# Eighteen products of the last output projection moved into the last slot, their bank, and the queue of the last sums

## The chip, the cores and the metric

One Trainium2 chip, one core. The metric is the device time in microseconds (us) of one execution of the program. Before the change three runs gave 1958.81, 1959.34 and 1960.34 us, a median of 1959.34 us. Engines are named as in the profile: PE (TensorE), PEld (its weight loads), DVE (VectorE), ACT (ScalarE), POOL (GpSimd), SP (SyncE, here only a DMA queue).

## The reference

Two attention blocks read the same input x (2048 x 512, 32 heads of 16) and are mixed row by row with a gate. Cut to what matters:

```
g = sigmoid((x * gate_w).sum(-1))
# A: causal softmax attention inside each of 4 segments of 512 rows, mixed with a linear memory of the earlier segments
o = sigmoid(beta) * a_mem + (1 - sigmoid(beta)) * softmax(q k^T / 4 + mask) v
a = o @ A_wo
# B: full softmax attention over 2048 keys
b = (softmax(q k^T / 4) v) @ B_wo
out = g * a + (1 - g) * b
```

The last output projection is the product of the normalised, gated o of both blocks (512 + 512 columns) with A_wo and B_wo.

## The kernel before

**Units and slots.** Attention is cut into 64 units: 32 of A (4 segments x 8 quarters of the heads, unit k) and 32 of B (4 chunks of 512 query rows x 8 quarters of 4 heads, unit 32 + k). Slot k of the main loop (L932 to L966) does B's unit 32 + k and A's unit k. In a slot, n runs over 37 groups (NG): groups 0 to 31 are B's, two per key tile of 128 keys, and 32 to 36 are A's. A group (`t_group`, L516) makes two score tiles of 128 x 512 on PE, one for each half of the array's rows, into two PSUM banks, and ACT takes the exponential of each tile out of its bank (L534) into `raw`. `pv` (L540) then multiplies the exponentials with the values and adds up in the bank `pvb`; in slot 31 (L860) it does so once per key tile, after the odd group, one key tile behind. The instructions of every engine stand in the order in which this code issues them.

**Banks.** PSUM has eight banks here: `tb` (two, TB), `mb`, `pvb`, and `sbk` (two tiles of two banks). `bank` (L88) hands out the allowed bank that was used longest ago. In slots 0 to 30 the scores use T3 = TB + [MB], and `sbk` holds other score tiles, of which only the row maximum is taken (L452 to L476, reduced on DVE). Slot 31 has no next unit to take maxima for, so its groups rotate over five banks, T3 and the first halves of the two `sbk` tiles (L934). The small jobs (`misc`, L95) also take theirs from T3: in slot 31 these are two halves of an earlier output projection, `out_mm(22)` after group 1 and `out_mm(23)` after group 28 (12 products each, L616, taken out by ACT L620 and by DVE L623), and `m_rows` (L501) after group 24.

**Output.** Each sum o·W is made of three products of split operands (high and low parts, TERMS). For the last 512 rows (c = 3), the tail does the projection: t counts four tiles of 128 rows, `tail_mm(t, gs, a)` (L639) adds the products of head groups gs and block a (0 is A, 1 is B) into the bank TAIL[t]. Of its 24 products a tile, 18 (head groups 0 to 2) need nothing of the last slot; their operands are split on DVE during the slot's first groups (L911). The other 6 need group 3, which waits for the units 63 and 31.

**The end of the last units.** `fin_copy` (L553) copies `pvb` to `pvs` (ACT L559) and stores it to DRAM (L561). For unit 63 the sums are loaded again (L567, L569), inverted on DVE (L574, L578), stored (L580) and loaded back in 64 rows (L586, `d<-rd`); POOL multiplies (L590), then SP loads the memory part (L593, `d<-om`). For unit 31, SP loads the denominators (L971) and sums (L972); the loop at L983 inverts and multiplies on DVE (L986 to L988), adds the memory part on POOL (L989), and splits (ACT L634, POOL L637). B's group 3 is split on DVE (L636, L637) at L980. `tail_out` (L646) copies the four banks out by halves and stores them.

## Time and profile before

| | us |
|---|---|
| median of three runs | 1959.34 |
| the profiled execution, its own time | 1956.4 |
| its span in the profile | 1954.7 |
| last slot, from its first score tile to the last product of pvb | 1883.69 to 1928.25 |
| tail, from there to the last product on PE | 1928.25 to 1950.76 |
| last copy out of PSUM and last stores | 1950.86 to 1954.7 |

The profiled execution took 1956.4 us, 1.7 us more than its span, and lay 2.9 us under the median of the runs. Times in rows are us from the start of the span. A row of the chain of waits says where the path to the last instruction ran; a row of the timeline says when an instruction started, how long it took, and in square brackets how long its engine had been idle and which instruction ended that. Matmul rows merge several instructions (x4); their ends overlap with the next row's start.

### The profile page before, as it was taken

The numbers are of one execution on the slowest core, as the hardware profiler recorded it, in microseconds if no ns is written. First come the engines' busy times: TensorE is split into PE (matmuls) and PEld (weight loads), VectorE is DVE, ScalarE is ACT, GpSimd is POOL, SyncE is SP. The second block draws the span as 40 slices with busy tenths as digits, with TensorE's granted clock in tenths as the row PEclk, the third lists the DMA queues.
The fourth block names the chain that finished last, engine by engine and source line by source line (L and its number), as shares of the span: only waits on it lengthen the run. The fifth ranks groups of instructions, "written<-read, shape, count | busy, mean of one in ns | idle before, by whom it ended". The sixth has DMA issues, their size and how long they took to land.

```text
span 1954.7 us, 43539 instructions
## 1 busy us (share of the span) xinstructions
PE 1930.3 (99%) x17485; PEld 939.3 (48%) x17485; DVE 1629.9 (83%) x1798; ACT 1433.4 (73%) x2699; POOL 275.8 (14%) x497
## 2 busy tenths in 40 slices
PE   7999999999999999999999999999999999999999
PEld 5887777444344444444444444444444444444445
DVE  7135766899999999999999999999999999999942
ACT  4233333688888888888888888888888888888884
POOL 5201000012120101111111111111111111111022
PEclk9999999999999999999999999999999999999999
DMA  7666655644444444343435453444354444434111
GB/s 218 170 205 188 198 192 178 156 98 115 98 115 93 106 91 109 81 111 80 114 87 115 87 115 87 113 87 115 87 115 87 109 86 96 101 88 106 48 50 58
DMA packets 163790, 222.49 MB, mean 114 GB/s; under 512 B 39916, under 2 KB 90556, under 8 KB 157828
## 3 DMA queue, kind: packets, MB, share of 16 engines
q1 hardware_dynamic: 159284, 211.41, 43.7%
q0 software_dynamic: 3248, 8.03, 2.1%
q8 instruction: 138, 2.26, 0.5%
q14 instruction: 64, 0.52, 0.1%
q10 hardware_dynamic: 1056, 0.26, 0.1%
HBM read 147.95 MB, written 68.16 MB: 111 GB/s over the span
## 4 chain that ended last, share of the span: by engine, by line
PE 95%; DVE 3%; ACT 1%; SPq 1%; DMA 1%; issue 0%; DVEq 0%; ACTq 0%
PE pvb L550 33%; PE tb L528 17%; PE sbk L474 12%; PE mb L528 9%; PE tb L304 4%; PE sbk L452 3%; PE tb L616 2%; PE mb L304 2%; PE sbk L287 1%; DVE mxb L476 1%; PE tb L287 1%; PE pvb L304 1%; PE mb L616 1%; PE sbk L456 1%; PE mb L287 1%; PE pvb L287 1%
## 5 line engine op out<-in xcount | busy, mean ns | idle before, releaser
L476 DVE TENSOR_REDUCE mxb<-sbk 128x2 f32<-128x1024 f32 x1024 | 1222.3, 1222 | 67.3 <-PE sbk L474 63.1
L534 ACT ACTIVATE raw<-tb 128x512 f32<-128x512 f32 x1555 | 887.5, 598 | 152.9 <-PE tb L528 89.6
L550 PE MATMUL pvb<-raw,vb 128*17 128x256 f32 (+1 forms) x8072 | 639.3, 388 | 0.0
L534 ACT ACTIVATE raw<-mb 128x512 f32<-128x512 f32 x782 | 467.6, 598 | 79.5 <-PE tb L528 44.8
L528 PE MATMUL tb<-qb,xh 64*128 64x512 f32 x872 | 331.6, 495 | 1.7 <-ACT raw L534 1.7
L550 PEld LDWEIGHTS pvb<-raw,vb 128*17 128x17 f32 x8072 | 134.4, 95 | 340.1 <-issue 336.6
L474 PE MATMUL sbk<-xh,qb 64*128 64x512 f32 x1344 | 281.5, 395 | 2.7 <-DVE mxb L476 1.8
L528 PE MATMUL mb<-qb,xh 64*128 64x512 f32 x445 | 220.6, 496 | 0.0
L537 POOL TENSOR_SCALAR_AFFINE_SELECT raw<-raw 128x256 f32<-128x256 f32 (+1 forms) x320 | 115.5, 361 | 709.6 <-ACT raw L534 701.7
L528 PEld LDWEIGHTS tb<-qb,xh 64*128 64x128 f32 x872 | 124.7, 183 | 179.6 <-issue 89.9
L528 PE MATMUL tb<-qb,kb 64*128 64x512 f32 x470 | 179.5, 496 | 1.3 <-DVE st L314 0.8
L460 DVE TENSOR_REDUCE mx<-sbk 128x2 f32<-128x768 f32 (+1 forms) x128 | 136.7, 1090 | 22.9 <-PE sbk L456 18.3
L474 PE MATMUL sbk<-kb,qb 64*128 64x512 f32 x704 | 146.4, 398 | 0.0
L474 PEld LDWEIGHTS sbk<-xh,qb 64*128 64x128 f32 x1344 | 138.3, 186 | 7.4 <-DVE mxb L476 5.0
L528 PEld LDWEIGHTS mb<-qb,xh 64*128 64x128 f32 x445 | 81.3, 183 | 95.2 <-issue 50.4
L590 POOL TENSOR_TENSOR o<-o,d 128x512 f32<-128x512 f32 x31 | 39.7, 1281 | 545.6 <-DMA d<-rd 461.9
L528 PEld LDWEIGHTS tb<-qb,kb 64*128 64x128 f32 x470 | 68.2, 183 | 100.1 <-issue 52.6
L528 PE MATMUL mb<-qb,kb 64*128 64x512 f32 x234 | 116.1, 496 | 0.0
L550 PE MATMUL pvb<-raw,va 128*17 128x256 f32 (+2 forms) x1280 | 94.7, 384 | 0.8 <-ACT pvs L559 0.8
L452 PE MATMUL sbk<-ka,qa 64*128 64x256 f32 (+3 forms) x512 | 88.2, 358 | 1.1
L528 PE MATMUL tb<-qa,ka 64*128 64x512 f32 (+3 forms) x339 | 79.5, 372 | 0.0
L311 ACT ACTIVATE st<-tb 128x512 fp32r<-128x512 f32 x33 | 19.8, 599 | 80.2 <-DVE phi L310 40.5
(284 smaller groups left out, 1837.6 us busy)
## 6 DMA issues: line engine op xcount, KB each, us to landing
xh<-dB SPq DMA_DIRECT2D x38, 512.0 KB
vb<-vdB SPq DMA_DIRECT2D x16, 1088.0 KB
dB<-st SPq DMA_DIRECT2D x64, 256.0 KB
dA<-st SPq DMA_DIRECT2D x64, 256.0 KB
pd<-pvs SPq DMA_DIRECT2D x64, 256.0 KB
kb<-dB SPq DMA_DIRECT2D x22, 512.0 KB
xh<-dB SPq DMA_DIRECT2D x38, 256.0 KB
qb<-dB SPq DMA_DIRECT2D x64, 128.0 KB
```

Source lines behind the costliest of these rows:

```text
L287: nc.tensor.matmul(b, lhs, WV[wi][:, k, :], start=n == 0, stop=n == 11)
L304: nc.tensor.matmul(b, WS[ws][w][wi][:, k, :], (XH, XL)[xi][c][:, k, :], start=n == 0, stop=n == 11)
L452: nc.tensor.matmul(b[:, j, c0:c0 + n], q_of(u)[r, p, i * 128:(i + 1) * 128], k_of(u, p)[r, :n], start=True, stop=False)
L460: nc.vector.tensor_reduce(m[:, :, p, i], b[:, :, :n], axis=AX.X, op=OP.max)
L474: nc.tensor.matmul(b[:, j], q_of(u)[r, p, i * 128:(i + 1) * 128], k_of(u, p)[r, kc * C:(kc + 1) * C], start=True, stop=True)
L476: nc.vector.tensor_reduce(MXB[u][:, :, p, i, kc], b, axis=AX.X, op=OP.max)
L528: nc.tensor.matmul(bs[j][:, c0:c0 + w], k_of(u, h // 2)[r, 128 * it:128 * it + 128], q_of(u)[r, h // 2, q0:], start=True, stop=True)
L534: nc.scalar.activation(pt, bs[j], AF.Exp, scale=SCALE)
L537: nc.gpsimd.affine_select(out=m, in_=m, pattern=[[1, 128]] if n < 2 else [[0, 2], [1, 128]], compare_op=OP.is_ge, fill=0.0, base=0, channe ...
L550: nc.tensor.matmul(PVB[32 * h:32 * h + E + 1, q0 + lo:q0 + hi], vt[:, it, 4 * q + h, :], pt[:, lo:hi], start=it == 0 and lo == 0, stop=it ...
L590: nc.gpsimd.tensor_tensor(o, o, d, op=OP.mult)
L616: nc.tensor.matmul(b, (AT["oh"], AT["ol"])[oi][:, g, a], (AT["wh"], AT["wl"])[wi][:, g, a], start=n == 0, stop=n == 11)
```

## The change

Three things, all of them in the last slot and behind it:

1. Tile t = 0 of the last projection gets `mb` as its bank, and its first 18 products run inside slot 31, six of them (one head group, both blocks) between the two score groups of a key tile, at n = 8, 14 and 20. The score groups of slot 31 rotate over four banks in place of five, without `mb`, and the small jobs of that slot over TB alone.
2. The store of unit 31's `pvs` and the two loads behind it are issued by ACT's queue, not SP's.
3. DVE normalises tiles 0 and 1 of unit 31 ahead of splitting B's group 3; the normalising of tiles 2 and 3 lies between those splits.

```
-        nc.sync.dma_start(AT["pd", u].rearrange("h r t -> (h r) t"), ps)
+        (nc.scalar if u == 31 else nc.sync).dma_start(AT["pd", u].rearrange("h r t -> (h r) t"), ps)
...
-    TAIL = T3 + [SBK[0][:, 0]]
+    TAIL = [MB] + TB + [SBK[0][:, 0]]
...
+        if k == 31:
+            for g in range(3):
+                pre[8 + 6 * g] = [todo(tail_mm, 0, (g,), a) for a in range(2)]
...
-        banks = T3 + [b[:, 0] for b in SBK] * (k == 31)
+        banks = T3 if k < 31 else TB + [b[:, 0] for b in SBK]
+        if k == 31:
+            mode["misc"] = TB
...
-    nc.sync.dma_start(den, AT["pd", 31][:, E:E + 1].to_broadcast([4, E, C]))
-    nc.sync.dma_start(AT["o"][1][64:, 3, 0], AT["pd", 31][:, :E])
-    for t in range(2):
+    nc.scalar.dma_start(den, AT["pd", 31][:, E:E + 1].to_broadcast([4, E, C]))
+    nc.scalar.dma_start(AT["o"][1][64:, 3, 0], AT["pd", 31][:, :E])
+    for t in range(1, 4):
         for a in range(2):
             tail_mm(t, range(3), a)
-    for a in range(2):
-        tail_mm(2, range(3), a)
     fin_norm("B", 3, 3)
+
+    def last_norm(t):
+        d = den[:, t * 128:(t + 1) * 128]
+        o = o_cols(3, t)[64:, 3, 0]
+        nc.vector.reciprocal(d, d)
+        nc.vector.tensor_tensor(d, d, AT["grest"][:, t * 128:(t + 1) * 128], op=OP.mult)
+        nc.vector.tensor_tensor(o, o, d, op=OP.mult)
+
+    def last_add(t):
+        o = o_cols(3, t)[:, 3, 0]
+        nc.gpsimd.tensor_tensor(o, o, AT["d"][1][:, t * 128:(t + 1) * 128], op=OP.add)
+        tail_split(t, slice(3, 4), 0, nc.gpsimd)
+
+    for t in range(2):
+        last_norm(t)
     for t in range(4):
         tail_split(t, slice(3, 4), 1)
-    for a in range(2):
-        tail_mm(3, range(3), a)
-    for t in range(4):
-        d = den[:, t * 128:(t + 1) * 128]
-        o = o_cols(3, t)[:, 3, 0]
-        nc.vector.reciprocal(d, d)
-        nc.vector.tensor_tensor(d, d, AT["grest"][:, t * 128:(t + 1) * 128], op=OP.mult)
-        nc.vector.tensor_tensor(o[64:], o[64:], d, op=OP.mult)
-        nc.gpsimd.tensor_tensor(o, o, AT["d"][1][:, t * 128:(t + 1) * 128], op=OP.add)
-        tail_split(t, slice(3, 4), 0, nc.gpsimd)
+        if t < 2:
+            last_add(t)
+        else:
+            last_norm(t)
+            last_add(t)
```

Behind that point the file's lines shift: what was L971, L972, L986 to L989 in the kernel before is L976, L977, L986 to L988 and L992 in the changed one.

**PE at the start of slot 31.** The rows are `out_mm(22)` (L616) behind group 1, and the score groups 2 and 3 behind it (L528); tb_110 and tb_111 are the two banks of TB, sbk_114 and sbk_115 the two halves of `sbk`. Before:

```order
L528 MATMUL tb_111<-qb_68,xh_87 128x512
L528 MATMUL tb_110<-qb_68,xh_87 128x512
L616 MATMUL mb<-wh,oh 128x512 x4
L616 MATMUL mb<-wl,oh 128x512 x4
L616 MATMUL mb<-wh,ol 128x512 x4
L528 MATMUL sbk_114<-qb_68,xh_87 128x512
L528 MATMUL sbk_115<-qb_68,xh_87 128x512
L528 MATMUL tb_111<-qb_68,xh_87 128x512
L528 MATMUL tb_110<-qb_68,xh_87 128x512
```

The changed kernel at the same place:

```order
L528 MATMUL tb_111<-qb_68,xh_87 128x512
L528 MATMUL tb_110<-qb_68,xh_87 128x512
L616 MATMUL tb_111<-wh,oh 128x512 x4
L616 MATMUL tb_111<-wl,oh 128x512 x4
L616 MATMUL tb_111<-wh,ol 128x512 x4
L528 MATMUL sbk_114<-qb_68,xh_87 128x512
L528 MATMUL sbk_115<-qb_68,xh_87 128x512
L528 MATMUL tb_110<-qb_68,xh_87 128x512
L528 MATMUL tb_111<-qb_68,xh_87 128x512
```

`out_mm(22)` moved from the free `mb` to tb_111, the bank that group 1 has just filled, and group 3 takes that bank again.

**PE at the first insertion.** The rows are groups 8 and 9 of the changed kernel, the `pv` of key tile 3 and groups 10 and 11:

```order
L528 MATMUL sbk_114<-qb_68,xh_87 128x512
L528 MATMUL sbk_115<-qb_68,xh_87 128x512
L643 MATMUL mb<-wh,kb_89 128x512
L643 MATMUL mb<-wl,kb_89 128x512
L643 MATMUL mb<-wh,kb_89 128x512 x2
L643 MATMUL mb<-wl,kb_89 128x512
L643 MATMUL mb<-wh,kb_89 128x512
L528 MATMUL tb_110<-qb_68,xh_87 128x512
L528 MATMUL tb_111<-qb_68,xh_87 128x512
L550 MATMUL pvb<-raw_86,vb_2773 17x512 x4
L528 MATMUL sbk_114<-qb_68,xh_87 128x512
L528 MATMUL sbk_115<-qb_68,xh_87 128x512
```

Six products stand between the two groups, and the even groups now always use the two `sbk` banks, the odd ones the two of TB, until `m_rows` shifts them by one bank.

**SP and ACT behind the slot.** SP's queue before, from the store of unit 63's sums on:

```order
L561 DMA pd_19419<-pvs 128x512
L567 DMA o_2775<-pd_19419 64x1x512
L569 DMA rec<-pd_19419 128x1x16
L580 DMA rd_19466<-rec 128x16
L561 DMA pd_19474<-pvs 128x512
L586 DMA d_2779<-rd_19466 64x1x512
L971 DMA d_2778<-pd_19474 64x1x512
L972 DMA o_2775<-pd_19474 64x1x512
L593 DMA d_2779<-om_2582 128x512
```

ACT's instructions in the changed kernel, from its last copy of `pvb` on:

```order
L559 ACTIVATE pvs<-pvb 128x512
L561 DMA pd_19492<-pvs 128x512
L976 DMA d_2778<-pd_19492 64x1x512
L977 DMA o_2775<-pd_19492 64x1x512
L634 CAST kb_89<-o_2775 128x128 x2
```

The store of unit 31's sums and both loads left SP's queue, where they stood behind the store of `rec` and around the load `d<-rd`, and stand on ACT right behind the copy that they wait for.

## The prediction

> **What bounds the kernel now.** I read the busy times first, then the chain of waits over the last 70 us, then the timelines of ACT, SP, DVE and POOL there, since the change touches nothing earlier. PE is busy through the whole span:
>
> ```profile
> span 1954.7 us, 43539 instructions
> PE 1930.3 (99%) x17485; PEld 939.3 (48%) x17485; DVE 1629.9 (83%) x1798; ACT 1433.4 (73%) x2699; POOL 275.8 (14%) x497
> ```
>
> So work that is only moved from one place on PE to another gains nothing unless PE waits at the new place. The chain of waits through the last slot shows how much it waits (start, us, what). A key tile is two score groups (L528) and eight matmuls of `pv` (L550):
>
> ```profile
> 1901.69 0.42 PE tb L528
> 1902.11 0.00 PE mb L528
> 1902.11 0.51 PE sbk L528 x2
> 1902.62 1.02 PE pvb L550 x8
> 1903.64 0.43 PE tb L528 x2
> ...
> 1910.95 0.98 PE pvb L550 x8
> ...
> 1914.02 3.01 PE tb L616 x12
> ...
> 1919.11 0.98 PE pvb L550 x8
> ```
>
> One key tile takes 1903.64 - 1901.69 = 1.95 us. Its bare work is 0.43 + 0.43 + 0.98 = 1.84 us (a pair of tiles takes 0.43; `pv` takes 0.98 where nothing holds it). So PE waits for about 0.11 us per key tile, and the row of its weight loads says for whom, a bank that ACT has not yet emptied:
>
> ```profile
> 1902.12 0.18 PEld L528 LDWEIGHTS sbk<-qb,xh 64*128 64x128 f32 x1 [0.21 <-ACT raw L534]
> ```
>
> ACT's timeline gives its side. These rows are, in order, group 1's exponentials and the copy of `out_mm(22)`; two places five exponentials apart in the steady part; one that runs alone; the first behind `out_mm(23)`; the last copy of `pvb`:
>
> ```profile
> 1885.33 1.11 ACT L534 ACTIVATE raw<-tb 128x512 f32<-128x512 f32 x2
> 1888.24 0.60 ACT L620 ACTIVATE yo<-mb 128x512 f32<-128x512 f32 x1 [1.81 <-PE mb L616]
> ...
> 1900.75 1.32 ACT L534 ACTIVATE raw<-sbk 128x512 f32<-128x512 f32 x2
> ...
> 1902.70 0.84 ACT L534 ACTIVATE raw<-mb 128x512 f32<-128x512 f32 x1
> 1903.18 1.34 ACT L534 ACTIVATE raw<-sbk 128x512 f32<-128x512 f32 x2
> ...
> 1912.39 0.60 ACT L534 ACTIVATE raw<-mb 128x512 f32<-128x512 f32 x1
> ...
> 1917.85 1.09 ACT L534 ACTIVATE raw<-sbk 128x512 f32<-128x512 f32 x2 [2.41 <-PE sbk L528]
> ...
> 1928.36 0.60 ACT L559 ACTIVATE pvs<-pvb 128x512 f32<-128x512 f32 x1 [1.25 <-issue]
> ```
>
> Exponentials follow each other every (1903.18 - 1900.75) / 5 = 0.486 us, four of them 1.94 us: ACT sets the pace in the steady part, and PE is 6% quicker. And where 12 products (3.01 us) came between two groups, ACT ran dry for 2.41 us: only about 0.6 us of such a block lies beside banked work.
>
> Behind the slot PE is alone on the path. The chain of waits from the last `pv` to the end, with `out_mm(22)` of the slot's start, used below, ahead of it:
>
> ```profile
> 1885.11 3.10 PE mb L616 x12
> ...
> 1928.25 8.57 PE tb L643 x36
> 1936.82 4.18 PE mb L643 x18
> 1941.00 4.19 PE sbk L643 x18
> 1945.19 2.79 PE tb L643 x12
> 1947.98 1.40 PE mb L643 x6
> 1949.37 1.39 PE sbk L643 x6
> 1950.86 0.44 DVE raw L654
> ```
>
> No gap: 96 products, 18 in 4.18 us, 0.232 us each. From the last product's end, 1950.76, to the DVE copy are 0.10 us, which I use as the hand-over between any two engines.
>
> **Part 1, what the tail loses.** The 18 products of t = 0 leave a stretch that is PE from end to end: **-4.18 us**, if PE still finds the operands of the last 24 in time (part 4).
>
> **Part 2, what the slot gains.** I step PE and ACT through the slot by hand with the durations above: 0.43 for a group, 0.98 for `pv`, 1.40 for six products, 0.486 from one exponential to the next, 0.60 from its start to its end, 0.10 for a hand-over. For the kernel before, this gives 1920.23 for the end of key tile 14's `pv` where the trace has 1919.11 + 0.98 = 1920.09, so the steps hold. For the changed one:
>
> - `out_mm(22)` now writes tb_111, the first bank of group 1. Before, it began at 1885.11. Now it waits for the first of the two exponentials that start at 1885.33: until 1885.33 + 0.60 + 0.10 = 1886.03. **+0.92 us.**
> - Group 3 needs that bank again for its second tile, so for the copy L620 to end: 0.10 + 0.60 + 0.10 = 0.80 behind the products, of which group 2 hides 0.43: **+0.37 us.**
> - With four banks, the second tile of an odd group waits for the last exponential of the odd group before it. Where ACT has caught up, the four exponentials of a key tile start 0.10, 0.59, 1.07 and 1.56 us behind the first group's end, so the last bank is free at 2.26; PE comes to it at 0.43 + 0.98 + 0.43 = 1.84. That is a wait of 0.42 us in place of 0.11. Up to group 8 the steps give **+0.27 us**, since ACT still has a stock there.
> - Each block of six products (groups 8 to 13, 14 to 19, 20 to 25): the block itself costs 1.40; the key tile behind it has no bank wait (ACT caught up during the block), the one after has the 0.42, and the block's own key tile none. Against three waits of 0.11: 1.40 + 0.42 - 0.32 = 1.50 each, and the third 1.56 with `m_rows` in it: **+4.56 us.**
> - From group 26 on both kernels are bound by PE and A's groups have the banks they need: nothing more.
>
> Sum of the slot: 0.92 + 0.37 + 0.27 + 4.56 = **+6.1 us**. Both ends: if the four banks cost nothing and the products used up all of PE's waits between groups 4 and 26 (about 1.1 us), 4.18 - 1.1 = +3.0. If a bank comes free only after the 0.84 us that an exponential lasts in the steady part (row 1902.70), the same steps give +7.2. I stay at 6.1, since the 0.60 of the row that runs alone fits an ACT that has caught up.
>
> The Trainium skill (Perfetto Trace Analysis, section "Matmul Optimizations") asks to use all eight PSUM banks, which speaks against taking `mb` from the scores. The wait of 0.21 us for a bank with five of them agrees. By that rule the products alone, with five banks kept and `out_mm(22)` in `mb`, would cost the slot 4.3 us by the same steps and the change would come out at about zero; what the banks add is the other 1.8 us.
>
> **Part 3, ACT's queue.** SP's timeline, DMA issues only:
>
> ```profile
> 1930.53 0.32 SPq L580 DMA_DIRECT2D rd<-rec  x1
> 1930.95 0.38 SPq L561 DMA_DIRECT2D pd<-pvs  x1
> 1931.99 0.53 SPq L586 DMA_DIRECT2D d<-rd  x1
> 1933.06 0.51 SPq L971 DMA_DIRECT2D d<-pd  x1
> 1933.62 0.51 SPq L972 DMA_DIRECT2D o<-pd  x1
> 1936.93 0.32 SPq L593 DMA_DIRECT2D d<-om  x1
> ```
>
> `pvs` was ready at 1928.36 + 0.60 = 1928.96, but its store stood behind that of `rec` until 1930.95. On ACT nothing stands before it: store at 1929.0, landing 2.1 us later (1930.95 to 1933.06), loads at 1931.1 and 1931.6, 2.0 us sooner. Behind the waiting loads on ACT's queue stand only the casts L634, which need their data anyway. This moves nothing on PE's path by itself: the price is 0, and it is the cover for part 4.
>
> **Part 4, whether the last 24 products find their operands.** The last steps of units 63 and 31 on POOL, with ACT's last cast (the second row of L989 is the next round):
>
> ```profile
> 1935.62 1.29 POOL L590 TENSOR_TENSOR o<-o,d 128x512 f32<-128x512 f32 x1 [8.04 <-DMA d<-rd]
> ...
> 1940.60 0.46 POOL L989 TENSOR_TENSOR o<-o,d 128x128 f32<-128x128 f32 x1 [3.69 <-DVE o L988]
> ...
> 1942.25 0.46 POOL L989 TENSOR_TENSOR o<-o,d 128x128 f32<-128x128 f32 x1 [0.23 <-DVE o L988]
> ...
> 1946.07 0.30 ACT L634 CAST xh<-o 128x128 fp32r<-128x128 f32 x1 [1.37 <-POOL o L989]
> ...
> 1946.45 0.46 POOL L637 TENSOR_TENSOR xh<-o,xh 128x128 fp32r<-128x128 f32 x1 [0.41 <-ACT xh L634]
> ```
>
> In the old clock, PE ends its 54 products at 1928.25 + 12.55 = 1940.8 and wants the last split of t = 3 at about 1946.2; POOL gave it at 1946.91, which is too late, so the reordering is needed. A round on POOL now takes 1942.25 - 1940.60 = 1.65 us, since it waits for DVE, 0.23 us each. With DVE's first two tiles ahead of its other work, on loads issued 2 us sooner, POOL can start when `d<-om` is there, about 2.1 us behind 1936.93, at 1939.0. A round without DVE in it is then 1.65 - 0.23 = 1.42 us, at least 0.46 + 0.30 (ACT) + 0.46; four, with some slack, end at 1944.8, 1.4 us early. What can spoil this is the DMA. The packets of 1934 to 1936 and 1936 to 1938:
>
> ```profile
> DMA packets 80, 0.16 MB, mean 78 GB/s; under 512 B 4, under 2 KB 4, under 8 KB 80
> ```
> ```profile
> DMA packets 76, 0.15 MB, mean 74 GB/s; under 512 B 4, under 2 KB 4, under 8 KB 76
> ```
>
> These are the 64-row loads L586, L971 and L972, one after the other at 39 rows per us, 1.65 us each. The change puts two of them ahead of or beside `d<-rd`. If the two queues take turns, `d<-rd` lands up to 1.6 us later, POOL's rounds end at 1946.4, and PE waits for 0 to 0.7 us. I take **+0.3 us**.
>
> The Trainium skill (DMA: Bandwidth & Descriptors, section "Issuing engines are not separate DMA queues") says that DMAs of all issuing engines interleave on the same 16 DMA engines, and that a second issuer saves only issue time. The store waited 2.0 us for SP's order here, which is more than the rule's saving; but by the rule the loads slow each other, which would make the +0.3 a 0.7.
>
> **Sum.** +6.1 - 4.2 + 0.3 = **+2.2 us**. On the profiled execution 1956.4 + 2.2 = 1958.6; on the median, which lay 2.9 above it, 1959.34 + 2.2 = **1961.5 us**. A difference of 0.2%, 3.9 us, is about what a measurement of this kernel can tell from no change, so this counts as no change.
>
> **Rivals.**
>
> - *The products fill PE's waits.* For it: PE waits 0.11 us per key tile, and a block also swallows the bank wait beside it. Against it: there are only 1.1 us to fill. +3.0 - 4.2 = -1.2, 1958.1 us. Chance 0.09.
> - *The slot takes the products for nothing*, because ACT and not PE paces it: -4.2, 1955.1 us. It needs a PE idle for a tenth of the slot; the 2.41 us of dry ACT behind a 3.01 us block speak against it. Chance 0.05.
> - *The tail doesn't shorten* (slower). Mechanism: `d<-rd` shares its DMA engines with the two loads that now go ahead, POOL's L590 starts late, the load `d<-om` behind it, and the last splits of POOL; PE waits at the first products of L643 that need them. It decides from the point where L590 starts more than 1.4 us later than now against the end of `pv`; each us beyond costs a us, up to 4.2: +6.1, 1965.4 us, in the full case. It counts as slower if over 2.0 us of the tail's gain go. For it: 1.6 us of delay are possible. Against: that leaves only 0.2. Chance 0.13, with the slot's upper end of +7.2 in it.
>
> The forecast (between 0 and +3.9) keeps 0.73.
>
> **How the numbers follow.** The range goes from the first rival, 1958.3 with the scatter of the runs, to +3.0 of slot excess and 0.7 lost in the tail and some scatter of the runs, 1964.0. Faster 0.05 (second rival), slower 0.13 (third), same 0.82.
>
> **What would show it.** Right: the last `pv` ends at about 1934.3; ACT shows a gap behind each block; PE waits for ACT's exponentials at every second or third odd group, 0.4 us each; `out_mm(22)` starts 0.9 us later; L643 x54 is followed by the last 24 with at most 0.7 us of gap; the end of PE is 2 us later. Wrong: the slot grows by less than 4 us (the bank waits are no waits), or L643 stands waiting for POOL L637 by over a microsecond (part 4 is wrong).

## The result, and the profile after

The changed kernel is slower: a median of 1965.01 us (22 runs) against 1959.7 us of the kernel before (22 runs, the three shown above among them). The ratio is **1.0025, 95% interval 1.0018 to 1.0032**, some 5 us. One of the 22 runs took 2727.83 us at a granted clock of 0.56; the ratio leaves it out, and the median of the other 21 is 1964.84 us. The prediction was 1961.5 us, between 1958.3 and 1964.0, which counted as no change; the measured time lies above that range. Its profiled execution took 1962.77 us, 6.37 more than that of before, and its page begins:

```profile
span 1961.1 us, 43525 instructions
...
PE 1933.0 (99%) x17485; PEld 940.4 (48%) x17485; DVE 1629.9 (83%) x1798; ACT 1433.7 (73%) x2699; POOL 275.8 (14%) x497
```

PE has as many matmuls as before. Its busy time tells nothing of the 6.4 us, so I cut the end of the program at two rows of ACT that every kernel has: the copy L609 shortly after the last slot's start, and the last L559, the copy of unit 31's `pvb`. **Slot** is from the one to the other, **tail** from there to the end of the span. The part ahead of the slot varies by up to 6 us from run to run (L609 starts at 1883.4 to 1889.5 us), while slots of one kind agree to 0.1 us; single runs are therefore compared by slot and tail, not by their spans. A span is printed to 0.1 us, so a tail is good to 0.05.

| us | before | after | change |
|---|---|---|---|
| slot | 44.94 | 51.25 | +6.31 |
| last L559 to the last product's end on PE | 22.39 | 20.94 | -1.45 |
| from there to the end | 3.95 | 5.52 | +1.57 |

The slot's growth is what was predicted (+6.1). The tail was to lose 3.9 us and is 0.1 us longer.

**The slot.** The chain of waits, with `out_mm(22)` (L616) ahead and then three key tiles, the first with a block of six products in it:

```profile
1885.96 3.02 PE tb L616 x12
...
1895.21 0.42 PE sbk L528 x2
1895.63 1.60 PE mb L643 x6
1897.23 0.43 PE tb L528 x2
1897.66 0.98 PE pvb L550 x8
1898.64 0.43 PE sbk L528 x2
1899.08 0.24 PE tb L528 x2
1899.32 0.98 PE pvb L550 x8
1900.30 0.44 PE sbk L528 x2
1900.75 0.97 PE tb L528 x2
1901.72 0.98 PE pvb L550 x8
1902.70 0.42 PE sbk L528 x2
```

The second key tile runs without a wait, 1.66 us, since ACT emptied its banks during the block. The third has the wait for a bank: its group of `tb` takes 0.97 in place of 0.43. Three key tiles take 1902.70 - 1895.21 = 7.49 us where they took 3 x 1.96 = 5.87. ACT shows the gap behind the block, and the copy of `out_mm(22)` that group 3 waits for:

```profile
1889.01 0.60 ACT L620 ACTIVATE yo<-tb 128x512 f32<-128x512 f32 x1 [2.62 <-PE tb L616]
...
1897.69 1.09 ACT L534 ACTIVATE raw<-tb 128x512 f32<-128x512 f32 x2 [0.93 <-PE tb L528]
```

**The tail on PE.** PE no longer runs from end to end. It stops three times before the last products (its timeline; in brackets the idle time and what ended it):

```profile
1947.97 0.50 PE L643 MATMUL mb<-wh,kb 128*128 128x512 f32 x1 [0.69 <-DVE kb L636]
...
1949.65 0.50 PE L643 MATMUL mb<-wh,kb 128*128 128x512 f32 x1 [0.72 <-ACT kb L634]
...
1954.55 0.51 PE L643 MATMUL sbk<-wh,xh 128*128 128x512 f32 x1 [0.37 <-ACT xh L634]
```

That is 1.78 us of waits. With the slow product behind each and smaller gaps, the starts of these products give 2.7 us: the 4.18 of the 18 products less the 1.45 that PE ends sooner. What came late is in the chain of waits (the transfer of `d<-rd`, POOL's L590, the load `d<-om`) and in DVE's timeline:

```profile
1938.33 6.29 DMA d<-rd
...
1944.70 1.30 POOL o L590
1946.02 2.64 DMA d<-om
```
```profile
1944.89 1.25 DVE L988 TENSOR_TENSOR o<-o,d 64x128 f32<-64x128 f32 x1 [2.76 <-DMA o<-pd]
...
1947.68 0.23 DVE L636 CAST kb<-o 128x128 fp32r<-128x128 f32 x1
...
1953.33 0.29 DVE L988 TENSOR_TENSOR o<-o,d 64x128 f32<-64x128 f32 x1
1953.65 0.42 DVE L654 COPY raw<-mb 128x256 f32<-128x256 f32 x1
```

From the issue of `d<-rd` to the start of L590 it took 1935.62 - 1931.99 = 3.63 us before, 1944.70 - 1938.33 = 6.37 us now. The load `o<-pd`, issued at 1938.54, also landed only at about 1944.85. DVE now takes its work in the order norm 0, norm 1, B's splits (L636), so it stood 2.76 us at norm 0, and the first split of B began 13.04 us behind the last L559, where before it was 8.58 (1936.94 - 1928.36). The copies out of PSUM stand behind all four norms on DVE, as they did before; here that put the first copy of `mb` (L654) at 1953.65, though PE had finished that bank by 1950.7.

**Behind PE.** The copies of three tiles came out together, and the eight stores were issued in one row, 0.50 us each. SP's timeline before, and then after:

```profile
1947.14 4.98 SPq L655 DMA_DIRECT2D out_dram<-raw  x8
```
```profile
1954.11 3.97 SPq L655 DMA_DIRECT2D out_dram<-raw  x8
```

Before, issuing ended at 1952.12, 0.41 us behind the last copy's end (1951.71); now it ends at 1958.08, 1.55 us behind it (1956.53). This lag looks like the cause of the 1.57 us, but it isn't, as the runs with two queues show below. What ends the changed kernel is POOL. These are its last instruction, and its instructions of the program's closing line, first before (L1017), then after (L1030):

```profile
1954.57 0.46 POOL L637 TENSOR_TENSOR xh<-o,xh 128x128 fp32r<-128x128 f32 x1 [0.41 <-ACT xh L634]
```
```profile
L1017 POOLq DRAIN  x3: 46/102/5735, 1946.4 to 1954.4; - x3
```
```profile
L1030 POOLq DRAIN  x3: 46/102/5733, 1954.5 to 1960.8; - x3
```

The three numbers are the shortest, the median and the longest in ns. A DRAIN belongs to the closing of the program and isn't counted as busy. The first of the three starts with POOL's last L637 and takes 5.73 us, to 1960.27; the other engines' closing follows, and the span ends at 1961.1, 6.0 us behind that L637 (1955.03). SP had seen the last store land by 1959.8. Before, the last L637 ended at 1946.91 (its row is in the prediction), POOL's DRAIN at 1952.1, and the span at 1954.7, 7.8 us behind L637: there the last stores closed the program, and POOL had some 1.75 us to spare. Against the last L559, POOL's last L637 ends 20.39 us behind it now and 18.55 before, so 1.84 us later. Less the 1.75, that is the 0.1 us by which the tail is longer.

### The profile page after: what moved, and what is told of

Same layout as the page of the kernel before. It is cut to its first block, busy times and chain, and to the rows that moved or that the text cites. A ratio compares the mean times of both kernels' runs of the same rounds, so it can differ in the third digit from the quotient of the medians.

```text
span 1961.1 us, 43525 instructions
## 1 busy us (share of the span) xinstructions
PE 1933.0 (99%) x17485; PEld 940.4 (48%) x17485; DVE 1629.9 (83%) x1798; ACT 1433.7 (73%) x2699; POOL 275.8 (14%) x497
## 4 chain that ended last, share of the span: by engine, by line
PE 93%; DVE 3%; DMA 1%; ACT 1%; issue 1%; SPq 1%; POOL 0%; DVEq 0%; POOLq 0%; ACTq 0%
PE pvb L550 33%; PE tb L528 17%; PE sbk L474 12%; PE mb L528 9%; PE tb L304 4%; PE sbk L452 3%; PE tb L616 3%; PE mb L304 2%; PE sbk L287 1%; PE pvb L304 1%; PE tb L287 1%; DVE mxb L476 1%; PE mb L616 1%; PE sbk L456 1%; PE mb L287 1%; PE pvb L287 1%
## 5 line engine op out<-in xcount | busy, mean ns | idle before, releaser
L534 ACT ACTIVATE raw<-mb 128x512 f32<-128x512 f32 x768 | 457.6, 596 | 79.2 <-PE tb L528 46.2
L528 PE MATMUL tb<-qb,xh 64*128 64x512 f32 x877 | 332.9, 495 | 1.8 <-ACT raw L534 1.7
L528 PE MATMUL mb<-qb,xh 64*128 64x512 f32 x433 | 215.1, 497 | 0.0
L528 PEld LDWEIGHTS tb<-qb,xh 64*128 64x128 f32 x877 | 125.5, 183 | 178.0 <-ACT raw L534 89.1
L528 PE MATMUL tb<-qb,kb 64*128 64x512 f32 x470 | 179.7, 496 | 1.3 <-DVE st L314 0.8
L528 PEld LDWEIGHTS mb<-qb,xh 64*128 64x128 f32 x433 | 79.2, 183 | 91.3 <-issue 48.6
L590 POOL TENSOR_TENSOR o<-o,d 128x512 f32<-128x512 f32 x31 | 39.7, 1281 | 551.4 <-DMA d<-rd 486.3
L528 PE MATMUL mb<-qb,kb 64*128 64x512 f32 x234 | 116.2, 497 | 0.0
L528 PEld LDWEIGHTS tb<-qb,kb 64*128 64x128 f32 x470 | 68.3, 183 | 100.0 <-issue 52.6
L528 PE MATMUL tb<-qa,ka 64*128 64x512 f32 (+3 forms) x343 | 79.2, 372 | 0.0
```

The source lines that it names most:

```text
L528: nc.tensor.matmul(bs[j][:, c0:c0 + w], k_of(u, h // 2)[r, 128 * it:128 * it + 128], q_of(u)[r, h // 2, q0:], start=True, stop=True)
L534: nc.scalar.activation(pt, bs[j], AF.Exp, scale=SCALE)
L590: nc.gpsimd.tensor_tensor(o, o, d, op=OP.mult)
```

## Experiments

The theory: the slot is as forecast (banks and blocks), and the tail's gain is eaten by the other two parts of the change (in the order of the section on it: 1 the products, 2 the queue, 3 DVE's order). The loads on ACT's queue slow `d<-rd`, and DVE's new order puts B's splits and the copies behind unit 31's late loads. The first half of this held; the runs show DVE's order and the end in another light. A rival: the tail would not have shortened anyway, since POOL's rounds end too late for 78 products, whatever parts 2 and 3 do. A second question beside it is whether the 1.6 us behind PE are the stores' issue on one queue. The measures of all runs, in us ("POOL's end" is the end of its last L637, behind the last L559):

| kernel | parts | slot | issue of `d<-rd` to L590 | POOL's end | tail | slot + tail |
|---|---|---|---|---|---|---|
| before | - | 44.94 | 3.63 | 18.55 | 26.34 | 71.28 |
| after | 1, 2, 3 | 51.25 | 6.37 | 20.39 | 26.46 | 77.71 |
| p1_only | 1 | 51.27 | 3.63 | 18.65 | 24.65 | 75.92 |
| p12 | 1, 2 | 51.24 | 6.25 | 21.06 | 27.04 | 78.28 |
| p13 | 1, 3 | 51.26 | 3.72 | 20.31 | 26.34 | 77.60 |
| p23_only | 2, 3 | 44.98 | 6.88 | 20.70 | 26.76 | 71.74 |
| own_bank | after, five score banks | 50.26 | 6.67 | 20.44 | 26.46 | 76.72 |
| banks_only | after, no product in the slot | 47.09 | 6.47 | 20.55 | 26.55 | 73.64 |
| two_queues | after, stores on two queues | 51.25 | 4.13 | 18.52 | 24.52 | 75.77 |
| no_o_load | after, without `o<-pd` | 51.24 | 4.25 | 16.96 | 22.98 | 74.22 |
| p1_2q | 1, stores on two queues | 51.24 | 3.52 | 18.44 | 24.44 | 75.68 |
| p1_skew | 1, copies earlier | 51.20 | 3.68 | 19.26 | 25.31 | 76.51 |
| six_banks | after, six score banks | 64.87 | 6.45 | 20.51 | 26.57 | 91.44 |
| combo | 1, six banks, two queues | 64.87 | 3.39 | 18.34 | 24.39 | 89.26 |
| fill_wait | before, 6 products in waits | 46.28 | 3.37 | 17.38 | 24.94 | 71.22 |
| extra_loads | before, 3 more loads | 44.95 | 3.96 | 22.58 | 28.63 | 73.58 |
| w36 | before, 3 products in a wait | 44.95 | 3.73 | 18.70 | 25.69 | 70.64 |

In 14 of these kernels the tail is POOL's end and 6.0 us (5.98 to 6.07 in the table, by the rounding of the spans), whatever the queues of the stores and wherever PE ended. Only before, fill_wait and w36, where POOL is done early against the stores, have 7.0 to 7.8. So the tail has to be read from POOL's last round.

### The parts, one by one

**p1_only**, part 1 alone, is the changed kernel with the edits of both p12 and p13, which follow. The first of them gives the three DMAs back to SP's queue, the other DVE its old order:

```
+        nc.sync.dma_start(AT["pd", u].rearrange("h r t -> (h r) t"), ps)
...
+    nc.sync.dma_start(den, AT["pd", 31][:, E:E + 1].to_broadcast([4, E, C]))
+    nc.sync.dma_start(AT["o"][1][64:, 3, 0], AT["pd", 31][:, :E])
...
+    for t in range(4):
+        last_norm(t)
+        last_add(t)
```

> Part 1 alone: the 18 products and their bank in the last slot; SP's queue and DVE's order as before. Theory A (the tail lost its gain to the loads on ACT's queue, which share DMA engines with d<-rd): d<-rd lands within 3.7 us of its issue again, the slot is still 6.3 us longer, the PE's end comes about 3.5 us sooner against the slot's end than before; span 1957.5 us. Theory B (DVE's order alone took the gain): the same span, since that is undone too. Theory C (the slot alone is the loss): span near the changed kernel's 1961.1.

Measured: slot 51.27, tail 24.65, timed at a ratio of 1.0019 (1.0006 to 1.0032). So part 1 alone makes the kernel slower: +6.33 in the slot, -1.69 in the tail. POOL's timeline has L590 as soon behind the issue (1938.47) as before:

```profile
1942.10 1.29 POOL L590 TENSOR_TENSOR o<-o,d 128x512 f32<-128x512 f32 x1 [8.13 <-DMA d<-rd]
```

Its PE ends 19.21 us behind the last L559, 3.18 sooner than before: the operands are late by 1.0 us, no more, without any cover. The tail gains only 1.69, since POOL's end stays where it was (18.65 for 18.55) and had no more than the 1.75 us to spare. The expected span of 1957.5 us was 3.6 us under the changed kernel's; by slot + tail the run lies 1.8 under it, half way between theories A and C.

**p12** is the changed kernel with DVE's old order:

```
-    for t in range(2):
-        last_norm(t)
...
-        if t < 2:
-            last_add(t)
-        else:
-            last_norm(t)
-            last_add(t)
+    for t in range(4):
+        last_norm(t)
+        last_add(t)
```

> Parts 1 and 2, DVE's order as before. Theory A: d<-rd still takes over 6 us to land, B's splits begin about 2.7 us later against the slot's end than before, the last products wait for POOL: PE's end is only about 0.8 us sooner than before against the slot's end; span about 1960. Theory B: span about 1957.5, as with part 1 alone.

Measured: tail 27.04, 2.39 more than p1_only. POOL's L590:

```profile
1946.93 1.29 POOL L590 TENSOR_TENSOR o<-o,d 128x512 f32<-128x512 f32 x1 [10.55 <-DMA d<-rd]
```

Part 2 by itself takes `d<-rd` from 3.63 to 6.25 us, and with DVE's order unchanged everything behind it shifts by that: from the start of L590 to POOL's end it is 11.3 us here, in p1_only and in the kernel before. So the loads' place on ACT's queue is the whole difference to p1_only. PE ends 22.48 us behind L559, where 0.8 us less than before (22.39) was expected.

**p13** is the changed kernel with SP's queue again:

```
-        (nc.scalar if u == 31 else nc.sync).dma_start(AT["pd", u].rearrange("h r t -> (h r) t"), ps)
+        nc.sync.dma_start(AT["pd", u].rearrange("h r t -> (h r) t"), ps)
...
-    nc.scalar.dma_start(den, AT["pd", 31][:, E:E + 1].to_broadcast([4, E, C]))
-    nc.scalar.dma_start(AT["o"][1][64:, 3, 0], AT["pd", 31][:, :E])
+    nc.sync.dma_start(den, AT["pd", 31][:, E:E + 1].to_broadcast([4, E, C]))
+    nc.sync.dma_start(AT["o"][1][64:, 3, 0], AT["pd", 31][:, :E])
```

> Parts 1 and 3, all three transfers on SP's queue. Theory A: d<-rd lands within 3.7 us; DVE waits for the denominators and sums instead, about 2 us, so B's splits are late by 3 to 4 us and the copies out of PSUM come behind the last normalising; span 1959 to 1960. Theory B: span near 1961, as the changed kernel, since DVE's order is kept.

Measured: tail 26.34, 1.69 more than p1_only. `d<-rd` is as quick as before (3.72), but DVE waits for the loads that now come behind it:

```profile
1948.82 0.95 DVE L986 RECIPROCAL d<-d 64x128 f32<-64x128 f32 x1 [7.34 <-DMA d<-pd]
...
1952.14 0.37 DVE L636 CAST kb<-o 128x128 fp32r<-128x128 f32 x1
```

B's split, whose operand POOL had finished at 1947.97, waits behind both norms until 1952.14. POOL's end comes 1.66 us later than in p1_only, and slot + tail (77.60) is the changed kernel's, as theory B had it, by the waits that theory A named. So on SP's queue part 3 costs 1.69. With both parts (the changed kernel) the loss against p1_only is 1.81, and 0.58 less than with part 2 alone: with the loads on ACT's queue DVE's new order helps a little, and the loss of the changed kernel is that of part 2.

**p23_only** leaves the 18 products in the tail:

```
-    TAIL = [MB] + TB + [SBK[0][:, 0]]
+    TAIL = T3 + [SBK[0][:, 0]]
...
-            for g in range(3):
-                pre[8 + 6 * g] = [todo(tail_mm, 0, (g,), a) for a in range(2)]
...
-        banks = T3 if k < 31 else TB + [b[:, 0] for b in SBK]
+        banks = T3 + [b[:, 0] for b in SBK] * (k == 31)
...
-    for t in range(1, 4):
+    for t in range(4):
```

> Parts 2 and 3 on the kernel before; no product moved. d<-rd takes over 6 us here too (theory A), but PE has 72 products to run and ends them 16.7 us behind the slot, by when all splits but the last are there: PE's end stays within 0.3 us of before and the span is 1954.7 +- 0.5. If theory C holds in the form that the slot is all there is, also 1954.7.

Measured: slot 44.98, tail 26.76, ratio 0.9997 (0.9988 to 1.0007). `d<-rd` takes 6.88 us here as well, and it costs little. PE's 72 early products last until B's first split is there, so PE ends where it did (22.39); POOL's end is 2.15 us later, of which 1.75 were to spare, and the tail is 0.42 longer. Of the rival half holds: without parts 2 and 3 PE does end 3.18 us sooner, but POOL's rounds let the tail gain no more than 1.69.

### Loads on two queues

**no_o_load** is the changed kernel without one of the two loads, and so without unit 31's sums:

```
-    nc.scalar.dma_start(AT["o"][1][64:, 3, 0], AT["pd", 31][:, :E])
```

> The changed kernel without the load of unit 31's sums (o<-pd), whose rows are left as they are: one of three 64-row loads is gone. Theory A (the three share the same DMA engines, 39 rows per us in all): d<-rd lands about 4.6 us behind its issue, where it took 6.3 with three and 3.6 alone; DVE's first normalising does not wait, B's splits begin 3 us sooner, and the tail is 24 us or less. Rival (issuing from ACT as such slows d<-rd): 6.3 us still.

Measured: `d<-rd` 4.25 us, tail 22.98, PE's end 18.22 behind L559, that is 4.17 sooner than before. The tail is 3.36 us shorter, since POOL ends 16.96 behind L559. With one load fewer beside `d<-rd` the whole 4.18 of the products came out on PE, and the wait of DVE for `o<-pd` is gone too, so the two are not told apart by this run.

**extra_loads** puts three loads of the same shape, whose data nothing reads, on ACT's queue of the kernel before:

```
+    for g in range(1, 4):
+        nc.scalar.dma_start(AT["o"][0][64:, g, 0], AT["pd", 63][:, :E])
```

> The kernel before with three more 64-row loads (of unit 63's sums, into rows that nothing reads any more) issued by ACT's queue right behind its last copy of pvb; nothing else is moved and no result changes. Theory A (64-row loads of both queues share DMA engines): d<-rd, which took 3.63 us from issue to POOL's L590, takes over 5 us, and den and sums land later too. Rival (the loads of the changed kernel were slow for another reason, such as their own order behind the store): 3.6 to 3.8 us.

Measured: `d<-rd` itself took 3.96 us, against the expectation: issued by 1931.13, at 1.65 us each, the three loads were through by then. They had met the transfer ahead of it. SP's timeline:

```profile
1931.36 0.32 SPq L580 DMA_DIRECT2D rd<-rec  x1
1931.77 0.38 SPq L561 DMA_DIRECT2D pd<-pvs  x1
1936.20 0.53 SPq L586 DMA_DIRECT2D d<-rd  x1
```

The small store `rd<-rec`, for which L586 waits, took 4.84 us to there, against 1.46 before (1930.53 to 1931.99). L590 began 4.0 us later against the last L559 than in the kernel before, POOL's end came as much later, and the tail is 2.29 us longer, the 4.03 less the 1.75. So 64-row loads on one queue do hold up a transfer of the other, with all else as before.

### The stores

**two_queues**:

```
-            nc.sync.dma_start(outr[tt * 128:(tt + 1) * 128, h], yo)
+            (nc.scalar if hf else nc.sync).dma_start(outr[tt * 128:(tt + 1) * 128, h], yo)
```

> The changed kernel with every second store of the tail (L655) issued by ACT's queue in place of SP's. Theory (eight stores at 0.49 us each on one queue, all behind DVE's late copies, end 1.6 us behind the last copy): from the last copy of pvb to the end 26.46 - 1.5 = 25.0 us, and the last store is issued within 0.6 us of the last copy. Rival (the stores' landing itself is slower, whatever queue): 26.4.

Measured: tail 24.52, but not for the reason tried: `d<-rd` landed in 4.13 us in this run, and POOL's end came 18.52 behind L559. The stores were issued as expected, the last one 0.38 us behind the last copy, where it was 1.55. Yet from PE's end to the span's end it took 5.44 us, as in the changed kernel (5.52). Why `d<-rd` was quick here, where the six other kernels with both loads on ACT's queue had 6.25 to 6.88, stays open.

**p1_2q** is p1_only with the same edit:

> Part 1 alone, as in the run p1_only (tail 24.65 us, of them 4.49 behind the last copy), with every second store of the tail on ACT's queue. Theory (the eight stores bunch on one queue behind DVE's late copies): tail 23.2 us, PE's end unchanged at 19.2 us behind the last copy of pvb, 3.0 us behind the last copy as in the kernel before. Rival (the extra 1.5 us is the landing of the stores): 24.6.

Measured: tail 24.44, the rival's number and not the theory's 23.2. It is 0.21 better than p1_only, as POOL's end is (18.44 for 18.65). ACT now issues between its copies, 0.38 and 0.34 us in turn (its timeline):

```profile
1955.82 0.38 ACT L652 ACTIVATE raw<-tb 128x256 f32<-128x256 f32 x1 [0.44 <-ACT raw L652]
1956.23 0.34 ACTq L655 DMA_DIRECT2D out_dram<-raw  x1
1956.61 0.38 ACT L652 ACTIVATE raw<-sbk 128x256 f32<-128x256 f32 x1 [0.41 <-ACT raw L652]
```

So the last copy ends 0.7 us later behind PE's end than in p1_only, but issuing ends only 0.38 us behind it, and 0.70 us sooner against L559 (21.01 for 21.71). From PE's end to the span's end it is 5.44 us in both: the stores came sooner and the end did not. With two_queues this refutes the issue on one queue as the cause of the 1.6 us.

**p1_skew** is p1_only with the first two tiles copied out behind the norms of tiles 2 and 3 instead of behind all:

```
-    for t in range(4):
-        last_norm(t)
-        last_add(t)
-    for t in range(4):
-        for a in (1, 0):
-            tail_mm(t, (3,), a)
-        tail_out(t)
+    for t in range(4):
+        last_norm(t)
+        last_add(t)
+        for a in (1, 0):
+            tail_mm(t, (3,), a)
+        if t > 1:
+            tail_out(t - 2)
+    for t in range(2, 4):
+        tail_out(t)
```

> Part 1 alone, with the copies out of PSUM of tile t placed behind the normalising of tile t + 2 on DVE instead of behind all of it. Theory (in p1_only the copies stood behind DVE's last normalising, so the eight stores came in one bunch, and their issue at 0.49 us each ended 1.5 us late): first store 1.5 us sooner against the last copy of pvb, 3.0 us behind the last copy, PE's end 0.4 us later than in p1_only (19.6), tail 23.6 us in place of 24.65. Rival (the end is set by the last product alone): 25.0.

Measured: tail 25.31, 0.66 worse than p1_only. The first store went out 1.5 us sooner against L559 (16.26 for 17.73), and issuing ended 0.57 us behind the last copy, so the lag of 1.55 is gone. Yet the span ended 3.98 us behind the last issue, where p1_only had 2.95 and before 2.58. The first copy, 0.42 us on DVE, now stands ahead of tile 3's norm, so POOL's last round, which waits for that norm, ends later (19.26 for 18.65), PE's end with it (19.82 for 19.21), and the span 6.0 us behind POOL. The rival's 25.0 was nearer than the theory's 23.6; the end hangs on POOL's last round, not on the stores.

### The banks

**banks_only** is the changed kernel with four banks, but all products in the tail:

```
-            for g in range(3):
-                pre[8 + 6 * g] = [todo(tail_mm, 0, (g,), a) for a in range(2)]
+            pass
...
-    for t in range(1, 4):
+    for t in range(4):
```

> The changed kernel with its 18 products back in the tail: four score banks and out_mm(22) in TB are what is left in the slot. Theory of the slot: 44.9 + 2.7 = 47.6 us, since the waits for a bank come every key tile without the products. Rival (only the products cost): 44.9. In the tail PE has 72 products again, so PE's end comes at 22.4 to 22.8 us behind the last copy of pvb, the end at 26.5 to 27.

Measured: slot 47.09, +2.15. Its chain of waits, two key tiles of the steady part:

```profile
1897.67 0.43 PE sbk L528 x2
1898.10 0.56 PE tb L528 x2
1898.65 0.98 PE pvb L550 x8
1899.63 0.43 PE sbk L528 x2
1900.07 0.68 PE tb L528 x2
1900.75 0.98 PE pvb L550 x8
1901.73 0.43 PE sbk L528 x2
```

A key tile takes (1901.73 - 1897.67) / 2 = 2.03 us against 1.96, so the steady price of the fifth bank is 0.07; 1.33 of the 2.15 are there by the first `pv` behind `out_mm(22)`, which sits in a bank of the scores (L620 starts 0.80 us later against L609 than before). The 18 products add 6.31 - 2.15 = 4.16 us to that, as much as they last back to back (4.18): the slot gave them no idle time.

**own_bank** gives the products the unused second half of an `sbk` tile and the scores their five banks:

```
-    TAIL = [MB] + TB + [SBK[0][:, 0]]
+    TAIL = [SBK[1][:, 1]] + TB + [SBK[0][:, 0]]
...
-        banks = T3 if k < 31 else TB + [b[:, 0] for b in SBK]
+        banks = T3 + [b[:, 0] for b in SBK] * (k == 31)
```

> The changed kernel, but the 18 products add up in the second half of sbk (unused in the last slot), so that the scores keep their five banks and out_mm(22) its mb. Measured from ACT's L609 to its last copy of pvb, the slot took 44.94 us before and 51.25 in the changed kernel. Theory of the slot (the products cost PE time and the lost bank costs waits): 44.9 + 4.3 = 49.2 us, about 2 us of the 6.3 gone. Rival (only the products cost): 51.2 still. The tail is as in the changed kernel, 26.5 us from the last copy of pvb to the end.

Measured: slot 50.26, 1.1 us more than expected. The waits of the slot's first half have a new row:

```profile
PEld sbk L643 <- ACT raw L534: 2.1, 2, 1.3
```

The products write one half of `sbk` and wait for ACT's exponentials, which read only its other half. So this doesn't price the lost bank cleanly.

**six_banks** lets the scores use both halves of both `sbk` tiles:

```
-        banks = T3 if k < 31 else TB + [b[:, 0] for b in SBK]
+        banks = T3 if k < 31 else TB + [b[:, j] for b in SBK for j in range(2)]
```

> The changed kernel with six score banks in the last slot (TB and both halves of both sbk tiles), so that mb is the only bank taken and the pairs rotate over three pairs of banks. Slot, from L609 to the last copy of pvb: before 44.94, changed 51.25. Theory (bank waits are part of it): 44.94 + 3 x 1.60 for the blocks + 0.9 for out_mm(22) in TB - 1.1 of PE's waits that are used up = 49.5 us. Rival (the products alone): 51.2.

Measured: slot 64.87, 13.6 us longer than with four banks. The chain of waits shows PE and ACT taking turns:

```profile
1903.02 0.47 PE sbk L528 x2
...
1903.97 0.60 ACT raw L534
...
1904.62 0.50 PE sbk L528
```

The group's second tile, in the other half, starts when ACT has emptied the first. Whether the chip or the order that the program sets makes the halves wait for each other, no run tells. And the windows (us, busy time of PE, PEld, DVE, ACT and POOL, granted clock, DMA share) show the granted clock of PE at 1.00 in the first of three windows with PE busy for 7.5 to 7.9 of 10 us, and at 0.68 and 0.84 in the other two:

```profile
1895.00:1905.00 10.00, 7.52 (x46) 2.79 (x46) 4.62 (x16) 6.54 (x13) 0.00 (x0) 1.00 0.06 18
1905.00:1915.00 10.00, 7.89 (x32) 2.86 (x28) 0.00 (x0) 5.32 (x10) 0.00 (x0) 0.68 0.01 2
1915.00:1925.00 10.00, 7.70 (x40) 2.75 (x40) 0.00 (x0) 6.41 (x12) 0.00 (x0) 0.84 0.00 0
```

**combo** puts part 1, those six banks, `out_mm(22)` in `mb` and stores on two queues together:

```
-        banks = T3 if k < 31 else TB + [b[:, 0] for b in SBK]
-        if k == 31:
-            mode["misc"] = TB
+        banks = T3 if k < 31 else TB + [b[:, j] for b in SBK for j in range(2)]
...
+            if (k, n) == (31, 2):
+                mode["misc"] = TB
```

> The repaired change: 18 products in the slot, six score banks, out_mm(22) in mb, SP's queue and DVE's order as before, every second store on ACT's queue. Slot 48.7 us, tail 23.2 us, together 71.9 where the kernel before has 71.3 and the changed one 77.7: the same as before within what a measurement tells. If moving products can gain at all, as the change supposes, it should be under 71.3.

Measured: slot 64.87 again, ratio 1.0082 (1.0066 to 1.0097). L620 was at its old place (4.82 us behind L609) in both, so `out_mm(22)` is no part of it; six_banks differs from the changed kernel in the banks alone, and they make the slot. The expectation of 48.7 us, which rested on them, falls.

### Products where PE does wait

Near the slot's end PE stands 0.82 us while ACT copies unit 63's `pvb`. **fill_wait** puts three products there and three more ahead of the `pv` of unit 31's third key tile, on the kernel before, with `mb` taken from the last five groups:

```
-    TAIL = T3 + [SBK[0][:, 0]]
+    TAIL = [MB] + TB + [SBK[0][:, 0]]
...
+        if k == 31:
+            pre[2 * NT + 2] = [todo(tail_mm, 0, (0,), 0)]
...
+            if (k, n) == (31, 2 * NT):
+                banks = TB + [b[:, 0] for b in SBK]
...
+    tail_mm(0, (0,), 1)
...
-            tail_mm(t, range(3), a)
+            tail_mm(t, range(0 if t else 1, 3), a)
```

> The kernel before with only six products moved, three each to the two places near the slot's end where PE waits with nothing to do (for the copy of pvb after group 34, and for POOL's masks ahead of the last pv); their bank is mb, which the groups 32 to 36 leave out. Theory (products are worth moving only into PE's waits): slot 45.0 to 45.3 us, PE's end 21.0 us behind the last copy of pvb where it was 22.39, tail 25.0 us; together about 1.0 us less than before, ratio 0.9995, too little to be told by the times. Rival (the tail is bound by the sums of the last units, not PE): tail 26.3, no gain.

Measured: slot 46.28, tail 24.94, together 0.06 less than before; ratio 0.9995 (0.9984 to 1.0007). PE's timeline:

```profile
1924.30 0.49 PE L528 MATMUL sbk<-qa,ka 64*128 64x512 f32 x2 [0.94 <-ACT raw L534]
```

The bank taken away cost a new wait of 0.94 at group 32, and the last three products filled nothing; the first three did vanish in the wait for L559.

**w36** puts three products alone at another place, behind group 36, where PE waits for POOL's masks ahead of the last three `pv`; it takes no bank away from the scores (the first half of an `sbk` tile, behind its last use):

```
-    TAIL = T3 + [SBK[0][:, 0]]
+    TAIL = [SBK[1][:, 0]] + T3[1:] + [SBK[0][:, 0]]
...
+        if k == 31:
+            pre[2 * NT + 4] = [todo(tail_mm, 0, (0,), 0)]
...
-            tail_mm(t, range(3), a)
+            tail_mm(t, range(0 if t or a else 1, 3), a)
```

> The kernel before with three products only, moved ahead of the last three pv of unit 31, where PE waits three times for POOL's masks (0.18 + 0.38 + 0.23 us); their bank is the first half of the second sbk tile, free by then. Theory (a product is free only where PE waits at that very place): slot 44.94 to 45.1 us, PE's end 21.7 where it was 22.39, tail 25.65, together 0.6 us less than before. Rival (every product costs its time in the slot, as in fill_wait): slot 45.6, together as before.

Measured: slot 44.95, tail 25.69: 0.64 us less than before, nearly the 0.70 of three products. PE's timeline at their place:

```profile
1931.21 0.50 PE L643 MATMUL sbk<-wh,kb 128*128 128x512 f32 x1
1931.54 0.40 PE L643 MATMUL sbk<-wl,kb 128*128 128x512 f32 x1
1931.78 0.40 PE L643 MATMUL sbk<-wh,kb 128*128 128x512 f32 x1
```

Its slot + tail, 70.64, is the smallest of all kernels here, and PE's end and the stores could come sooner because POOL had time to spare; 0.03% is too little for the times to tell, and its one time (1961.08 us) doesn't.

## Why the prediction was wrong, by its own steps

The parts here are those of the prediction, not those of the change.

- **Part 1** (18 products less in the tail, -4.18): the size was right on PE. no_o_load shows it whole, PE's end 4.17 us sooner. What the tail gains by it is bounded by POOL: 1.69 in p1_only.
- **Part 2** (the slot, +6.1): right, +6.31. By its terms: up to the first `pv` behind `out_mm(22)` +1.33 (forecast 0.92 + 0.37), from there to group 8 +0.06 (0.27), groups 8 to 26 +4.90 (4.56), behind them nothing. A block of six cost 1.60 among score groups, not the 1.40 of six back to back; the bank wait behind it was about as forecast (0.54 for 0.42).
- **Part 3** (ACT's queue, price 0): wrong. I looked at what the loads no longer wait for, and gave them no price of their own. p12 against p1_only: +2.39.
- **Part 4** (the last 24 products, +0.3, at most 0.7) is **the step that failed**. The tail was to be 3.9 us shorter and is 0.1 longer, 4.0 too much. In the prediction's own terms, POOL's last split was to end at 1944.8, 16.4 behind L559; it ended 20.4 behind it. Of these 4.0, 2.8 are `d<-rd`: I bounded its delay by one load, 1.6 us, though two loads of 1.65 go ahead. With both in front the bound from the same rows is 3.3 us, and six of the seven kernels with both loads on ACT's queue gave 2.6 to 3.3 (6.25 to 6.88, less the 3.63). Another 0.7 is the load `d<-om`: the first round of POOL (L992) came 2.80 us behind its issue, not 2.1. The last 0.4 are the four rounds, 6.2 us for 5.8, since the fourth waits 0.98 us for DVE's norm 3. The way of the loss was the third rival's ("the tail doesn't shorten", 1965.4 us, chance 0.13), whose chance rested on the bound of 1.6. Its own rule, 1.4 us of slack and a us for each beyond, would give 2.8 - 1.4 = 1.4 us of loss, since it took the 2.1 and the 5.8 as given.
- **The end behind PE** was not in the sum at all: I let it follow PE's last product. In the changed kernel it follows POOL's last split by 6.0 us. The forecast of 16.4 and these 6.0 make a tail of 22.4, just what PE's 3.9 gave, so with POOL in time the forecast would have come out by luck.
- **The first two rivals** (the products fill PE's waits, or are free) are refuted: 4.16 us for products that last 4.18.
- The rule that the prediction cited from the Trainium skill (DMA: Bandwidth & Descriptors, section "Issuing engines are not separate DMA queues") agrees with p12 and extra_loads: a second queue's loads slow the first one's. The 0.7 that I drew from it was again the bound of one load.

What stays open: `d<-rd` in 4.13 us in two_queues; what POOL's DRAIN does in its 5.73 us; and a clean price of a bank for the products alone, since both kernels made for it waited on halves of `sbk`.

## What to carry to other kernels

Before work is moved out of the last stretch of a program, ask which engine the end of the program hangs on, and how much time the others have to spare: here PE's 4.2 us could give at most 1.75 while POOL's last round stood where it was. Check it by what stays constant over several kernels (6.0 us behind POOL in 14 of 17), not by which engine ends last on the timeline. A load issued sooner on a second queue is a load that now runs beside another; bound its price by all the transfers put ahead, and look at what the in-order engines do while the slowed ones are out. Moved products pay only where PE's timeline shows an idle stretch with a bank to spare, and there a block as long as that stretch is all that fits.

## What the runs showed that I had not expected

- POOL's closing DRAIN took 5.73 us from the start of its last instruction in the kernels before and after, and 14 of 17 spans ended 6.0 us behind that instruction's end. Stores that came sooner did not move it.
- Two banks of one PSUM tile acted as one for waits: a slot of 51.2 us became 64.9, and the granted clock fell from 1.00 to 0.68 and 0.84 in windows where PE was busy for 7.7 to 7.9 of 10 us.
- Six full-row products between half-row score groups took 1.60 us, against 1.40 in a row of such products.
- Three small loads on ACT's queue stretched an 8 KB store of SP's queue, with its landing, from 1.46 to 4.84 us.
